# Linear attention and a sine MLP on one core: the first group's work in a new, written-out order, in eight single banks

## The chip, the core and the metric

The kernel runs on one core of a Trainium2 chip. The metric is the device time in microseconds (us), lower is better. The core's engines are TensorE (PE; PEld is its loading of weights), VectorE (DVE), ScalarE (ACT), GpSimd (POOL) and SyncE (SP). They run side by side, each through its own list of instructions in the order in which the program was written, and wait for one another by semaphores. DMA transfers are issued here by SP and by POOL.

## The reference

Two stages follow one another. The first is a causal linear attention with a decay for each head, over 4 batches, 8 heads, 768 positions and 64 values a head. The second is a two-layer MLP with a sine in it, over the resulting 3072 rows of 512 values.

```python
for b in range(nb):                          # blocks along the sequence
    intra = (qb @ kb.T * Dmask) @ vb         # within the block
    inter = (qb * lam_pow) @ kv_state        # from all blocks ahead
    out[:, :, sl] = intra + inter
    kv_state = lam_block * kv_state + (kb * rev_pow).T @ vb
...
x = attn_out, batch by batch, as 3072 x 512
h = x @ w_in                                 # 512 -> 2048
s = sin(alpha * h)
g = h + s * s / (alpha + 1e-9)
out = g @ w_out                              # 2048 -> 512
```

## The kernel before, in words

**Tiling.** The sequence is cut into six chunks of 128 positions. A *unit* u = 4 t + b is chunk t of batch b. The four units of a chunk make a *group* of 512 columns in the tile `xt`, and the MLP is done group by group. The 2048 inner features are 16 *sixteenths* of 128.

**A unit's attention** in the first two chunks: `transposes(u)` turns k and q by PE into PSUM and copies them out by ACT; `scores(u)` multiplies them by eight matmuls into `F_ps`, and DVE multiplies that by the decay mask `Cmask` into `STm`; the outputs are eight matmuls with v (`first_out` in chunk 0, `intra_mm` in chunk 1) plus four with the state `kv` (`inter_mm`, chunk 1 alone); DVE scales them into `xt` (`first_out` or `copy_x`). For the state, POOL decays k (`decay_k`), `state_mm` multiplies it with v, DVE copies the result into `kvs`, POOL casts it into `kv` (`state_put`) and decays it into `kvd` (`state_decay`). From chunk 2 on units are done in pairs: SP transposes k and q by DMA (`pair_transposes`), POOL decays k for both (`pair_decay`), and `pair_scores`, `pair_mask` and `pair_out` follow.

**A sixteenth of the MLP.** `hidden(g, f)` is four matmuls of 512 columns into one bank of PSUM and, on ACT, the sine; the square follows on ACT, or in group 0 on DVE where `on_act` says so (f = 0, 2, 4, 6). `finish(g, f)` is one scalar_tensor_tensor on DVE, which reads the same bank and writes `gall`; only then is the bank free. `project(g, n)` is one of 16 steps of the second layer, four matmuls of 512 columns each; step n works for batch m and a quarter (`part`) of the features and needs a quarter of `w_out`. In a step with part 3 ACT copies the rows out and SP stores them.

**The order.** Nothing is scheduled at run time: each engine's order is that in which the Python code emits. Group 0 is begun by a list of calls behind `spin` (PE kept busy with unused matmuls) and goes on in the main loop over g and i, where `slots(g)` says what of the next chunk's attention is done beside sixteenth i, and `feed(g)` which loads, state casts and decays POOL gets there. Behind the loop's pass g = 0 stand steps 0 to 3 of the projection; from g = 1 on each pass i does `hidden(g, i)` and then a projection step of the group before, four steps ahead (`LEAD`).

**PSUM** has eight banks of 512 float32. In the old kernel the tag `pf` holds a tile of two banks (`F_ps`, also `O_ps` of the pairs and `KVA_ps`); the others (`po`, `pqk`, `ops`, `h0`, `h1`, `h2`) are single. A tile of a tag waits until the last one's readers are done.

Of the kernel before, what the change touches and what calls it, by code (L numbers as in the profile page):

```python
# [14 lines left out]
def kernel(  # L15
# [197 lines left out]
    def transposes(u, tag="pqk"):  # L213
        t, b = divmod(u, B)
        QK_ps = psA.tile([P, 2, HP, T], BF16, name="QK_ps", tag=tag)
        for hp in range(HP):
            nc.tensor.transpose(out=QK_ps[:, 1, hp, :],
                                in_=kn[t][:, b, 2 * hp:2 * hp + 2, :], identity=iden[:])
        for hp in range(HP):
            nc.tensor.transpose(out=QK_ps[:, 0, hp, :],  # L220
                                in_=qn[t][:, b, 2 * hp:2 * hp + 2, :], identity=iden[:])
        QKT = qkp.tile([P, 2, HP, T], BF16, name="QKT")
        nc.scalar.copy(out=QKT[:], in_=QK_ps[:])  # L223
        st[u]["QT"], st[u]["KT"] = QKT[:, 0, :, :], QKT[:, 1, :, :]

    def scores(u, halves=1):
        QT, KT = st[u]["QT"], st[u]["KT"]
        F_ps = psA.tile([P, 2, HP, T], FP32, name="F_ps", tag="pf")
        for hp in range(HP):
            for hd in range(2):  # L230
                nc.tensor.matmul(out=F_ps[:, hd, hp, :],  # L231
                                 lhsT=KT[hd * D:(hd + 1) * D, hp, :],
                                 rhs=QT[hd * D:(hd + 1) * D, hp, :],
                                 start=True, stop=True)
        STm = work.tile([P, 2, HP, T], BF16, name="STm")
        n = HP // halves
        for s in range(halves):
            w = slice(s * n, (s + 1) * n)
            nc.vector.tensor_tensor(out=STm[:, :, w, :], in0=F_ps[:, :, w, :], in1=Cmask[:, :, w, :],  # L239
                                    op=ALU.mult)  # L240
        st[u]["STm"] = STm

    def state_mm(us, tag="pqk"):
        KVA_ps = psA.tile([P, 2, HP, D], FP32, name="KVA_ps", tag=tag)
        for n, u in enumerate(us):
            t, b = divmod(u, B)
            for hp in range(HP):
# [5 lines left out]
        for n, u in enumerate(us):  # L253
            t, b = divmod(u, B)
            kvs[u] = ksp.tile([P, HP, D], FP32, name="kvs")
            if t == 0:
                nc.vector.tensor_copy(out=kvs[u][:], in_=KVA_ps[:, n, :, :])
            else:
                nc.vector.tensor_tensor(out=kvs[u][:], in0=KVA_ps[:, n, :, :], in1=kvd[b][:], op=ALU.add)
# [14 lines left out]
    def intra_mm(u, bank="po"):  # L274
# [42 lines left out]
    def pair_scores(us, tag):  # L317

        F_ps = psA.tile([P, 2, HP, T], FP32, name="F_ps", tag="pf")
        G_ps = [psA.tile([P, HP, D], FP32, name="G_ps", tag=x) for x in ("po", tag)]  # L320
        for hp in range(HP):
            for c in range(2):
                for hd in range(2):
                    for n, u in enumerate(us):
                        w, s = slice(n * D, (n + 1) * D), slice(hd * D, (hd + 1) * D)
                        nc.tensor.matmul(out=G_ps[hd][w, hp, :] if c else F_ps[w, hd, hp, :],  # L326
# [9 lines left out]
    def pair_mask(us):  # L336
        nc.vector.tensor_tensor(out=st[us[0]]["ST"][0][:], in0=st[us[0]]["F_ps"][:], in1=Cmask[:], op=ALU.mult)  # L337

    def pair_out(us, tag):
# [3 lines left out]
        O_ps = psA.tile([P, 2, HP, T], FP32, name="O_ps", tag="pf")  # L343
# [12 lines left out]
        for c in range(2):  # L356
            for hp in range(HP):
                for n in range(2):
                    w = slice(n * D, (n + 1) * D)
                    for hd in range(2):  # L360
                        nc.tensor.matmul(out=O_ps[hd * D:(hd + 1) * D, n, hp, D * c:T],  # L361
                                         lhsT=vn[t][w, 2 * c + b, 2 * hp + hd, :], rhs=ST[c][w, hd, hp, :],
                                         start=(hp == 0 and c == 0), stop=False, skip_group_check=True)
        for n, u in enumerate(us):
            st[u]["O_ps"] = O_ps[:, n]
            for hp in range(HP):
                nc.tensor.matmul(out=O_ps[:, n, hp, :], lhsT=kv[u % B][:, hp, :, :], rhs=st[u]["QT"][:, hp, :],  # L367
                                 start=False, stop=(hp == HP - 1), skip_group_check=True)
            if tag:
                st[u]["K_ps"] = K_ps[n]  # L370

    def sum_state(u):
        if "K_ps" in st[u]:
            kvs[u] = ksp.tile([P, HP, D], FP32, name="kvs")
            nc.vector.tensor_tensor(out=kvs[u][:], in0=st[u]["K_ps"][:], in1=kvd[u % B][:], op=ALU.add)
# [7 lines left out]
    def on_act(g, f):  # L383
        return f % 2 == 1 or f > 7 if g == 0 else True

    FIRST = "h0 h2 po h1 ops h0 h2 h1 ops".split()

    def h_tag(g, f):
        return f"h{(g * NFC + f) % 3}"

    begun = {}

    def hidden(g, f, start_only=False):


        tag = FIRST[f] if g == 0 and f < len(FIRST) else h_tag(g, f)
        parts = [slice(0, GRP)]
        if (g, f) in begun:
            hps, parts = begun.pop((g, f)), [slice(GRP // 2, GRP)]
        else:  # L400
            hps = psA.tile([P, GRP], FP32, name="hps", tag=tag)
        if start_only:
            begun[g, f], parts = hps, [slice(0, GRP // 2)]
        for w in parts:
            for c in range(NDC):
                nc.tensor.matmul(out=hps[:, w], lhsT=w_in_of[f][:, c, :],  # L406
                                 rhs=xt[g][:, c, w], start=(c == 0), stop=(c == NDC - 1))
        if start_only:
            return
        s_sb = mlps.tile([P, GRP], BF16, name="s_sb")  # L410
        nc.scalar.activation(out=s_sb[:], in_=hps[:], func=ACTF.Sin, scale=alpha_sb[:, f:f + 1])  # L411
        s2 = mlps.tile([P, GRP], BF16, name="s2")
        if on_act(g, f):
            nc.scalar.activation(out=s2[:], in_=s_sb[:], func=ACTF.Square)  # L414
        hps_of[g, f] = (hps, s_sb, s2)

    def finish(g, f):
        hps, s_sb, s2 = hps_of.pop((g, f))
        if not on_act(g, f):
            nc.vector.tensor_tensor(out=s2[:], in0=s_sb[:], in1=s_sb[:], op=ALU.mult)  # L420
        nc.vector.scalar_tensor_tensor(out=gall[g][:, f, :], in0=s2[:], scalar=r_sb[:, f:f + 1],  # L421
                                       in1=hps[:], op0=ALU.mult, op1=ALU.add)
# [7 lines left out]
    def project(g, n):  # L430
        m, part = ORDER[n]
        if part == 0:
            ops_of[g, m] = psA.tile([P, DM], FP32, name="ops", tag=("ops", "pqk")[m % 2])
# [36 lines left out]
    def first_out(u, tag, hps_=range(4)):  # L470
# [6 lines left out]
        w = slice(hps_[0], hps_[-1] + 1)  # L477
        nc.vector.tensor_tensor(out=xt[0][:, w, u * T:(u + 1) * T], in0=O_ps[:, w, :],
# [8 lines left out]
    def half_T(u, nm, tag):  # L487

        src = {"KT": kn, "QT": qn}[nm]
        X_ps = psA.tile([P, HP, T], BF16, name="X_ps", tag=tag)  # L490
        for hp in range(HP):
            nc.tensor.transpose(out=X_ps[:, hp, :], in_=src[0][:, u, 2 * hp:2 * hp + 2, :], identity=iden[:])
        XT = firstp.tile([P, HP, T], BF16, name=nm)
        nc.scalar.copy(out=XT[:], in_=X_ps[:])
        st[u][nm] = XT[:]

    spin(9)
    half_T(0, "KT", "pqk")
    spin(3)
    half_T(0, "QT", "ops")  # L500
    spin(1)
    transposes(1, "po")
    spin(1)
    scores(0)
    a_ps = psA.tile([P, NFC], FP32, name="a_ps", tag="h2")
    nc.tensor.transpose(out=a_ps[:], in_=alpha_fp[:], identity=idf[:])
    for hp in range(HP):
        nc.scalar.activation(out=Etab[:, hp, :], in_=pos_row[:], func=ACTF.Exp, scale=ln_hd[:, hp:hp + 1])
    alpha_sb = consts.tile([P, NFC], FP32, name="alpha_sb")
    nc.vector.tensor_copy(out=alpha_sb[:], in_=a_ps[:])  # L510
    r_sb = consts.tile([P, NFC], FP32, name="r_sb")
    nc.vector.reciprocal(out=r_sb[:], in_=alpha_sb[:])
    spin(2)
    scores(1)
    spin(1)
    transposes(2, "pqk")
    spin(1)
    first_out(0, "po")
    spin(1)
    first_out(1, "h1")  # L520
    spin(1)
    scores(2)
    warm = consts.tile([P, 1], FP32, name="warm")
    nc.scalar.activation(out=warm[:], in_=lnlam[:, 0:1], func=ACTF.Sin)
    spin(1)
    half_T(3, "KT", "ops")
    spin(1)
    half_T(3, "QT", "h2")
    spin(1)
    first_out(2, "po")  # L530
    scores(3, 2)
    spin(3)
    first_out(3, "h1", range(0, 2))
    first_out(3, "ops", range(2, 4))
    hidden(0, 0, True)
    hidden(0, 1, True)


    def part_fo(uf, uo, bank="po"):

        if uo is not None:
            intra_mm(uo, bank)
        if uf is not None:
            scores(uf)
        if uo is not None:
            inter_mm(uo)

    def part_k(us, tag="pqk"):
        state_mm(us, tag)
        for u in us:  # L550
            if u >= B:
                state_put(u)
                state_decay(u)

    def slots(g):

        u = [B * (g + 1) + b for b in range(B)]
        T_, FO = transposes, part_fo
        if g == 0:
            return {}, {3: [(part_k, (0, 1), "pf")], 6: [(part_k, (2, 3), "pf")],  # L560
                    8: [(T_, u[0])], 9: [(T_, u[1], "po")], 10: [(FO, u[0], None)],
                    12: [(FO, u[1], u[0]), (copy_x, u[0])], 13: [(T_, u[2])],
                    14: [(FO, None, u[1]), (T_, u[3], "ops"), (copy_x, u[1])], 15: [(FO, u[2], None)]}, {}
# [24 lines left out]
    def feed(g):  # L588

        u = [B * (g + 1) + b for b in range(B)]  # L590
        if g == 0:
            return {7: [(state_put, 0), (state_put, 1)],
# [91 lines left out]
```

## Time and profile before

| | us |
|---|---|
| three runs | 214.43, 214.48, 215.0 (median 214.48) |
| the profiled execution | 214.55, of which the span of the profile is 212.8 |
| PE busy in the span | 203.8 (96%) |
| ACT, DVE, POOL busy | 146.7, 124.6, 106.0 |
| DVE idle ahead of L421 (finish), mostly for ACT | 63.0 |
| granted clock of PE, mean | 0.996 |

The times given with a row are from the start of the span. A row of the timeline has the start, the duration, the engine, the line, the operation, the tiles out<-in and a count; in brackets stands idle time ahead of it and what ended it. "PE busy" counts a matmul up to its modelled end, so neighbours overlap: four matmuls of a sixteenth show 1.03 us and start 0.86 us ahead of the next. The projection steps (L436) and the sixteenths (L406) make up most of PE's time. Loads by POOL's queue (q0) carry 13.4 MB in 77280 packets.

### The profile page before, as it was taken

What the parts mean: (1) busy time and instruction counts of PE and PEld (TensorE: products, weight loads), DVE (VectorE), ACT (ScalarE), POOL (GpSimd) and SP (SyncE); (2) the same over time, 40 slices, a digit from 0 to 9 for tenths busy, and PEclk for the clock granted to TensorE, in tenths of its full rate; (3) what the DMA queues carried; (4) which work ended last, traced back from release to release, by engine and by line L of the source; (5) the groups of instructions that cost most, each with busy time, mean ns of one, the idle gap of its engine ahead of it and who ended that gap; (6) DMA issues with size and microseconds to landing.
All of it is one profiled execution on the core that took longest, in us unless ns stands there. A gap on an engine that the chain in (4) does not pass through costs nothing.

```text
span 212.8 us, 4607 instructions
## 1 busy us (share of the span) xinstructions
PE 203.8 (96%) x1859; PEld 99.9 (47%) x1859; DVE 124.6 (59%) x193; ACT 146.7 (69%) x235; POOL 106.0 (50%) x148
## 2 busy tenths in 40 slices
PE   7799987999999999999999999999999999999993
PEld 2455444544445454454544454544454544444462
DVE  5686978844648764767644677744757544444200
ACT  4774999539685658767679667679677679878521
POOL 7999999896999999528389017110000000000000
PEclk9999999999999999999999999999999999999998
DMA  5999999999999999994999957951110102011032
GB/s 92 154 166 206 175 170 179 207 179 136 170 202 166 161 189 115 154 162 29 185 137 60 212 80 47 177 124 49 52 49 2 52 0 100 2 52 49 0 113 84
DMA packets 100373, 24.69 MB, mean 116 GB/s; under 512 B 92528, under 2 KB 97408, under 8 KB 100352
## 3 DMA queue, kind: packets, MB, share of 16 engines
q0 software_dynamic: 77280, 13.37, 81.3%
q1 hardware_dynamic: 23072, 11.03, 24.6%
q8 instruction: 14, 0.23, 0.4%
q14 instruction: 7, 0.06, 0.1%
HBM read 27.28 MB, written 6.29 MB: 158 GB/s over the span
## 4 chain that ended last, share of the span: by engine, by line
PE 81%; POOL 10%; DMA 6%; issue 1%; DVE 1%; ACT 0%; POOLq 0%; ACTq 0%
PE ops L436 37%; PE hps L406 34%; DMA qn<-in_q_dram 6%; POOL kn L99 2%; POOL vn L99 2%; PE O_ps L367 2%; POOL kdec L210 2%; POOL w_in L105 2%; PE hps L450 2%; PE O_ps L361 1%; POOL qn L99 1%; PE F_ps L326 1%; PE KVA_ps L352 1%; DVE STm L239 1%; PE O_ps L279 1%
## 5 line engine op out<-in xcount | busy, mean ns | idle before, releaser
L421 DVE SCALAR_TENSOR_TENSOR gall<-s,r_sb,hps 128x512 bf16<-128x512 bf16 x96 | 71.3, 746 | 63.0 <-ACT s L414 62.4
L411 ACT ACTIVATE s_sb<-hps,alpha_sb 128x512 bf16<-128x512 f32 x96 | 65.7, 686 | 46.5 <-PE hps L406 46.5
L406 PE MATMUL hps<-xt,w_in 128*128 128x512 bf16 (+1 forms) x392 | 97.6, 375 | 0.0
L436 PE MATMUL ops<-w_out,gall 128*128 128x512 bf16 x368 | 93.1, 379 | 0.1
L414 ACT ACTIVATE s<-s_sb 128x512 bf16<-128x512 bf16 x92 | 57.9, 630 | 2.9
L406 PEld LDWEIGHTS <-w_in 128*128 128x128 bf16 x392 | 37.4, 98 | 43.5 <-issue 1.7
L436 PEld LDWEIGHTS <-gall 128*128 128x128 bf16 x368 | 34.9, 98 | 39.7 <-DMA w_out<-in_moe_w_out_dram 0.2
L265 POOL CAST kv<-kvs 64x256 bf16<-64x256 f32 x40 | 16.2, 405 | 27.7 <-PE O_ps L367 20.8
L441 ACT COPY o_sb<-ops 128x512 f32<-128x512 f32 x23 | 13.1, 571 | 6.0 <-PE ops L436 6.0
L293 DVE TENSOR_TENSOR xt<-O_ps,Etab 128x512 bf16<-128x512 f32 x20 | 13.6, 686 | 4.2 <-PE O_ps L367 3.3
L95 POOL DMA_DIRECT2D kn<-in_k_dram x16 | 13.3, 848 | 0.0
L99 POOL DMA_DIRECT2D qn<-in_q_dram x10 | 12.9, 1288 | 0.8 <-DMA w_out<-in_moe_w_out_dram 0.8
L95 POOL DMA_DIRECT2D vn<-in_v_dram x16 | 13.2, 845 | 0.0
L302 POOL TENSOR_TENSOR kdec<-kn,Rpair 128x1024 bf16<-128x1024 bf16 x6 | 11.4, 1910 | 1.9 <-DMA kn<-in_k_dram 1.9
L485 PE MATMUL hps<-fill 128*128 128x512 bf16 x26 | 9.9, 476 | 1.5 <-DVE fill L125 1.5
L239 DVE TENSOR_TENSOR STm<-F_ps,Cmask 128x1024 bf16<-128x1024 f32 (+1 forms) x9 | 9.8, 1103 | 1.7 <-PE F_ps L231 1.5
L271 POOL TENSOR_TENSOR kvd<-kvs,L 128x256 f32<-128x256 f32 x16 | 9.8, 614 | 1.0
L337 DVE TENSOR_TENSOR STm<-F_ps,Cmask 128x1024 bf16<-128x1024 f32 x8 | 9.7, 1217 | 0.0
L210 POOL TENSOR_TENSOR kdec<-kn,Rtok 128x512 bf16<-128x512 bf16 x8 | 8.5, 1070 | 0.2
L223 ACT COPY QKT<-QK_ps 128x1024 bf16<-128x1024 bf16 x6 | 6.0, 1000 | 1.0 <-PE QK_ps L220 0.8
L334 DVE TENSOR_TENSOR STm<-G_ps,Cmask 128x256 bf16<-128x256 f32 x16 | 6.0, 419 | 0.6
L99 POOL DMA_DIRECT2D vn<-in_v_dram x6 | 6.0, 1021 | 0.0
(80 smaller groups left out, 115.3 us busy)
## 6 DMA issues: line engine op xcount, KB each, us to landing
out_dram<-o_sb SPq DMA_DIRECT2D x23, 256.0 KB, 2.4
vn<-in_v_dram POOLq DMA_DIRECT2D x20, 128.0 KB, 5.2
kn<-in_k_dram POOLq DMA_DIRECT2D x19, 128.0 KB, 5.9
w_out<-in_moe_w_out_dram POOLq DMA_DIRECT2D x4, 512.0 KB, 14.2
w_in<-in_moe_w_in_dram POOLq DMA_DIRECT2D x3, 512.0 KB, 11.1
qn<-in_q_dram POOLq DMA_DIRECT2D x3, 512.0 KB, 8.9
qn<-in_q_dram POOLq DMA_DIRECT2D x4, 256.0 KB, 12.4
w_in<-in_moe_w_in_dram POOLq DMA_DIRECT2D x2, 256.0 KB, 6.8
```

The source lines that it names most:

```text
L95: nc.gpsimd.dma_start(out=dst[t][n * D:(n + 1) * D, 2 * c:2 * c + 2, :, :].rearrange("p b h e -> p (b h) e"), in_=src[2 * n:2 * n + 2, :, ...
L99: nc.gpsimd.dma_start(out=dst[t][:, b0:b1, :, :].rearrange("p b h e -> p (b h) e"), in_=src[b0:b1, :, t * T:(t + 1) * T, :].rearrange("b h ...
L210: nc.gpsimd.tensor_tensor(out=kdec[:], in0=kn[t][:, b, :, :], in1=head_bc(Rtok), op=ALU.mult)
L239: nc.vector.tensor_tensor(out=STm[:, :, w, :], in0=F_ps[:, :, w, :], in1=Cmask[:, :, w, :], op=ALU.mult)
L265: nc.gpsimd.tensor_copy(out=kv[b][s, :, hd, :], in_=kvs[u][s, :, :])
L293: nc.vector.tensor_tensor(out=xt[t][:, :, b * T:(b + 1) * T], in0=st[u]["O_ps"], in1=Etab[:], op=ALU.mult)
L406: nc.tensor.matmul(out=hps[:, w], lhsT=w_in_of[f][:, c, :], rhs=xt[g][:, c, w], start=(c == 0), stop=(c == NDC - 1))
L411: nc.scalar.activation(out=s_sb[:], in_=hps[:], func=ACTF.Sin, scale=alpha_sb[:, f:f + 1])
L414: nc.scalar.activation(out=s2[:], in_=s_sb[:], func=ACTF.Square)
L421: nc.vector.scalar_tensor_tensor(out=gall[g][:, f, :], in0=s2[:], scalar=r_sb[:, f:f + 1], in1=hps[:], op0=ALU.mult, op1=ALU.add)
L436: nc.tensor.matmul(out=ops[:], lhsT=gall[g][:, f, m * P:(m + 1) * P], rhs=w_out_sb[part][:, f % 4, :], start=(f == 0), stop=(f == NFC - 1))
L441: nc.scalar.copy(out=o_sb[:], in_=ops[:])
```

## The change

1. The whole of group 0, its attention, chunk 1's attention, the states of chunk 0 and the first seven projection steps, is written as one string, `FILL`, of 168 entries. A loop emits them one by one; the helpers are split so that an entry is one engine's piece (matmuls, copy, mask, sine, square, finish). So the order on each engine is the string's.
2. All eight banks are single: `pf` becomes `pfa` and `pfb`, and each entry names its bank. `scores` and the pairs' `F_ps` and `O_ps` become lists of two tiles; a mask becomes two instructions of 128x512.
3. Sixteenths 0, 1 and, of group 1, 0, 1 and 2 (entries 16, 17, 18) are done in two halves of 256 columns: `Ha`, when the first two batches of `xt` are there, and `Hb`.
4. Which square goes to which engine changes: in group 0 nine on ACT and seven on DVE (0, 2, 3, 6, 7, 11, 12) for twelve and four; those of 16, 17 and 18 on DVE. Two of the four state copies of chunk 0 go to ACT.
5. POOL gets the four `w_out` loads ahead of all eight state casts (four of the eight stood ahead of them). The decays, the loads of chunk 2 and all behind it keep their order. SP's order is unchanged.
6. The main loop starts with g = 1; in it the passes i = 0, 1, 2 emit only their feeds, as their sixteenths and projection steps are in `FILL`. The banks of the later sixteenths rotate in another order (`h_tag`).

```diff
-    def scores(u, halves=1):
+    def scores(u, banks):
...
-        F_ps = psA.tile([P, 2, HP, T], FP32, name="F_ps", tag="pf")
+        F_ps = [psA.tile([P, HP, T], FP32, name="F_ps", tag=x) for x in banks]
...
+    def mask(u, w=slice(0, 4)):
+        for hd in range(2):
+            nc.vector.tensor_tensor(out=st[u]["STm"][:, hd, w, :], in0=st[u]["F_ps"][hd][:, w, :],
+                                    in1=Cmask[:, hd, w, :], op=ALU.mult)
...
+    def first_state(u, on_scalar):
+        kvs[u] = ksp.tile([P, HP, D], FP32, name="kvs")
+        (nc.scalar.copy if on_scalar else nc.vector.tensor_copy)(out=kvs[u][:], in_=st[u]["K_ps"])
...
     def pair_mask(us):
-        nc.vector.tensor_tensor(out=st[us[0]]["ST"][0][:], in0=st[us[0]]["F_ps"][:], in1=Cmask[:], op=ALU.mult)
+        for hd in range(2):
+            nc.vector.tensor_tensor(out=st[us[0]]["ST"][0][:, hd], in0=st[us[0]]["F_ps"][hd][:], in1=Cmask[:, hd],
+                                    op=ALU.mult)
...
-    def on_act(g, f):
-        return f % 2 == 1 or f > 7 if g == 0 else True
...
+    def hidden_mm(g, f, tag, w=slice(0, GRP)):
+
+        if tag:
+            hps_of[g, f] = psA.tile([P, GRP], FP32, name="hps", tag=tag)
+        for c in range(NDC):
+            nc.tensor.matmul(out=hps_of[g, f][:, w], lhsT=w_in_of[f][:, c, :],
+                             rhs=xt[g][:, c, w], start=(c == 0), stop=(c == NDC - 1))
...
+    FILL = """
+        Et F0:pfa,pfb spin2 M0 F1:po,ops Tk2:h2 spin3 Tq2 spin1 M1 cp2 I0:ops spin2 I1:h2 F2:po,pqk Tk3:h1
+        spin1 ck3 X1 Tq3:pfb spin3 M2 cq3 F3:h1,h2 X0 Mb3 I2:pfb spin3 Ma3 Ha1:po X2 Ib3:ops warm Ia3:h2
+        Ha0:pfa Xa3 AT:pfb Xb3 al Hb1 Hb0 H3:pqk sin1 sqA1 Z1 sin0 H2:h0 sin2 wout sqD2 sqD0 K2:pfb H4:ops
+        H6:h1 sin3 sqD3 Z0 H5:po ksA3 sin4 ksA2 sin6 Z2 sqA4 H7:pfb H8:pfa sin5 Z3 sqD6 Z4 sin7 Tk5:pqk
+        Tk4:ops sqA5 K0:h2 Tq5 sqD7 Z6 Z5 Z7 sin8 sqA8 Z8 cp5 Tq4 H10:h0 cp4 ksD0 put0 H11:po ksD1
+        F5:pfa,pfb sin11 F4:ops,pqk sin10 M5 H13:h1 H14:h2 put1 sin13 sqD11 sqA13 sqA10 M4 sin14 H15:pfa
+        sin15 I5:pqk Z11 Z13 sqA15 sqA14 I4:ops J5 J4 H9:pfb Tk7:h1 X5 Tk6:po Tq7 Tq6 X4 Ha18:pqk put3 cp7
+        Z15 Ha17:pfa Z14 cp6 sin9 F7:h2,ops Z10 H12:h1 F6:h0,po put2 sqA9 M7 I7:ops M6 P0:h2 I6:h0 Z9 J7 J6
+        X7 Ha16:pfb sin12 X6 sqD12 P1:po Hb17 Hb16 Z12 Hb18 sin17 P2 P3 sin16 sqD17 Z17 sqD16 sin18 sqD18
+        Z16 P4 P5 Z18 P6
+    """
...
+    rest = """decay 4, load 0 0, decay 5, load 0 2, kvd 0, load 1 0, kvd 1, decay 6, load 1 2, kvd 2, decay 7, kvd 3"""
...
-    for g in range(NT + 1):
-        if g < NT:
+    for g in range(1, NT + 1):
+        if 1 < g < NT:
...
+            if g == 1 and i < 3:
+                continue
```

The entries: F scores, M mask (Ma, Mb halves), T transposes of k or q, cp, ck and cq their copies, I the outputs' matmuls with v, J those with the state, X the scaling into `xt`, H a sixteenth's matmuls, sin and sq its sine and square (A on ACT, D on DVE), Z its finish, K the states of two units, ksA and ksD their copies, put the casts, P a projection step, wout the four loads, AT and al alpha, Et the powers, warm the loading of the sine's table.

More of the change, by code (lines that the diff above doesn't have):

```diff
@@ L234, in scores, with state_mm @@
                                  start=True, stop=True)
[L235 to L243, printed above, removed]
+        st[u]["F_ps"] = F_ps
+        st[u]["STm"] = work.tile([P, 2, HP, T], BF16, name="STm")
+    def mask(u, w=slice(0, 4)):
+        for hd in range(2):
+            nc.vector.tensor_tensor(out=st[u]["STm"][:, hd, w, :], in0=st[u]["F_ps"][hd][:, w, :],
+                                    in1=Cmask[:, hd, w, :], op=ALU.mult)
+    def state_mm(us, tag):
         KVA_ps = psA.tile([P, 2, HP, D], FP32, name="KVA_ps", tag=tag)
@@ L417, in finish @@
-    def finish(g, f):
[L418 to L422, printed above, removed]
+        return ("h2", "h1", "h0")[(g * NFC + f) % 3]
+    def hidden_mm(g, f, tag, w=slice(0, GRP)):
[4 more added lines that the diff above has]
+                             rhs=xt[g][:, c, w], start=(c == 0), stop=(c == NDC - 1))
@@ L424, with hidden @@
+    def hidden(g, f):
+        hidden_mm(g, f, h_tag(g, f))
+        sine(g, f)
+        square(g, f)
+    def finish(g, f):
+        nc.vector.scalar_tensor_tensor(out=gall[g][:, f, :], in0=s2_of.pop((g, f))[:], scalar=r_sb[:, f:f + 1],
+                                       in1=hps_of.pop((g, f))[:], op0=ALU.mult, op1=ALU.add)
     ops_of = {}
@@ L493, in half_T, with copy_half, powers @@
+    def copy_half(u, i):
+        nm = ("KT", "QT")[i]
         XT = firstp.tile([P, HP, T], BF16, name=nm)
-        nc.scalar.copy(out=XT[:], in_=X_ps[:])
+        nc.scalar.copy(out=XT[:], in_=st[u]["X_ps", i][:])
         st[u][nm] = XT[:]
+    def powers():
+        for hp in range(HP):
+            nc.scalar.activation(out=Etab[:, hp, :], in_=pos_row[:], func=ACTF.Exp, scale=ln_hd[:, hp:hp + 1])
+    alpha_sb = consts.tile([P, NFC], FP32, name="alpha_sb")
+    r_sb = consts.tile([P, NFC], FP32, name="r_sb")
@@ L497 @@
+    gall[1] = gbp.tile([P, NFC, GRP], BF16, name="gall")
+    new_xt(1)
     spin(9)
-    half_T(0, "KT", "pqk")
+    half_T(0, 0, "pqk")
+    copy_half(0, 0)
     spin(3)
-    half_T(0, "QT", "ops")
+    half_T(0, 1, "ops")
+    copy_half(0, 1)
     spin(1)
-    transposes(1, "po")
+    transposes(1, 0, "po")
+    transposes(1, 1)
+    copy_T(1)
     spin(1)
-    scores(0)
-    a_ps = psA.tile([P, NFC], FP32, name="a_ps", tag="h2")
-    nc.tensor.transpose(out=a_ps[:], in_=alpha_fp[:], identity=idf[:])
@@ L507 @@
[L507 to L546, printed above, removed]
@@ new lines, with at_group @@
+    """
+    half = (slice(0, GRP // 2), slice(GRP // 2, GRP))
+    two = (slice(0, 2), slice(2, 4))
+    def at_group(f):
+        return divmod(f, NFC)
+    DO = {
+        "spin": lambda n: spin(n), "Et": powers, "AT": alpha_T, "al": alpha_in, "warm": sine_table,
+        "wout": lambda: [load_w_out(i) for i in range(4)],
+        "ck": lambda u: copy_half(u, 0), "cq": lambda u: copy_half(u, 1), "cp": copy_T,
+        "Tk": lambda u, x: half_T(u, 0, x) if u == 3 else transposes(u, 0, x),
+        "Tq": lambda u, x=None: half_T(u, 1, x) if u == 3 else transposes(u, 1),
+        "F": lambda u, *x: scores(u, x), "M": mask,
+        "Ma": lambda u: mask(u, two[0]), "Mb": lambda u: mask(u, two[1]),
+        "I": lambda u, x: first_out(u, x) if u < B else intra_mm(u, x),
+        "Ia": lambda u, x: first_out(u, x, range(0, 2)), "Ib": lambda u, x: first_out(u, x, range(2, 4)),
+        "J": inter_mm, "X": lambda u: first_x(u) if u < B else copy_x(u),
+        "Xa": lambda u: first_x(u, two[0]), "Xb": lambda u: first_x(u, two[1]),
+        "Ha": lambda f, x: hidden_mm(*at_group(f), x, half[0]), "Hb": lambda f: hidden_mm(*at_group(f), None, half[1]),
+        "H": lambda f, x: hidden_mm(*at_group(f), x), "sin": lambda f: sine(*at_group(f)),
+        "sqA": lambda f: square(*at_group(f)), "sqD": lambda f: square(*at_group(f), False),
+        "Z": lambda f: finish(*at_group(f)),
+        "K": lambda u, x: state_mm((u, u + 1), x), "ksA": lambda u: first_state(u, True),
+        "ksD": lambda u: first_state(u, False), "put": state_put,
+        "P": lambda n, x=None: project(0, n, x),
+    }
@@ L611, in feed @@
                 14: [(Tr, t, 1), (pair_decay, nxt)]}
-    for g in range(NT + 1):
-        if g < NT:
+    rest = """decay 4, load 0 0, decay 5, load 0 2, kvd 0, load 1 0, kvd 1, decay 6, load 1 2, kvd 2, decay 7, kvd 3"""
+    entries = FILL.split()
+    last = max(n for n, e in enumerate(entries) if e[:3] in ("put", "wou"))
+    for n, entry in enumerate(entries):
+        if entry == "P6":
+            for a in feed(1)[0]:
+                a[0](*a[1:])
+        do(entry)
+        if n == last:
+            for a in rest.split(", "):
+                op, *x = a.split()
+                if op == "decay":
+                    decay_k(int(x[0]))
+                elif op == "kvd":
+                    state_decay(int(x[0]))
+                else:
+                    load_one(2, int(x[0]), int(x[1]), int(x[1]) + 2)
+    for g in range(1, NT + 1):
+        if 1 < g < NT:
             gall[g] = gbp.tile([P, NFC, GRP], BF16, name="gall")
```

155 lines of the change are left out of this document (62 added, 93 removed).

## The prediction

> **What bounds the kernel now.** I read the page first (busy shares, slices), then the windows by stage, the timeline of PE, POOL and DVE, and last the DMA issues with their times to landing.
>
> ```profile
> PE   7799987999999999999999999999999999999993
> POOL 7999999896999999528389017110000000000000
> DMA  5999999999999999994999957951110102011032
> ```
>
> The windows by stage (length, then busy time of PE, its weight loads, DVE, ACT and POOL, the granted clock, the DMA share and GB/s):
>
> ```profile
> 15.00:45.00 30.00, 27.30 (x261) 14.63 (x258) 23.65 (x37) 21.03 (x33) 28.48 (x36) 1.00 1.68 189
> 45.00:50.00 5.00, 5.00 (x25) 2.28 (x24) 1.82 (x3) 3.36 (x6) 4.64 (x11) 1.00 2.44 158
> 50.00:205.00 155.00, 155.00 (x1446) 73.74 (x1445) 88.75 (x134) 110.95 (x177) 59.07 (x82) 1.00 0.89 101
> ```
>
> From 45 us to 205 us PE has no idle time at all, and the change leaves that work and nearly all its order alone. So it can only win ahead of 45 us: the whole rest moves earlier by what the start saves, unless something in it does not move. What may not move is the DMA stream: its slices (5.3 us each) stand at 9 tenths up to about 95 us.
>
> The timeline of PE (start, duration):
>
> ```profile
> 49.90 1.03 PE L406 MATMUL hps<-xt,w_in 128*128 128x512 bf16 x4
> ...
> 66.50 0.45 PE L352 MATMUL KVA_ps<-vn,kdec 64*64 64x64 bf16 x32
> 66.77 0.52 PE L361 MATMUL O_ps<-STm,vn 64*64 64x128 bf16 x32
> ```
>
> That of POOL:
>
> ```profile
> 30.80 1.73 POOL L265 CAST kv<-kvs 64x256 bf16<-64x256 f32 x4
> ...
> 52.23 3.76 POOL L302 TENSOR_TENSOR kdec<-kn,Rpair 128x1024 bf16<-128x1024 bf16 x2 [1.92 <-DMA kn<-in_k_dram]
> 55.93 3.31 POOL L95 DMA_DIRECT2D vn<-in_v_dram  x4
> ```
>
> And the DMA issue that starts at 58.40, the last of the four v loads of chunk 2, with its time to landing:
>
> ```profile
> vn<-in_v_dram POOLq DMA_DIRECT2D x1, 128.0 KB, 7.9
> ```
>
> 49.90 is hidden(1, 3), the first step after everything that the change touches: both kernels have done the same work when PE gets there. 66.50 is the first use of v of chunk 2, in pair_out of the first pair. The last v load lands at 58.40 + 7.9 = 66.3, and PE comes to it 0.2 us later. That distance decides this change.
>
> **Part 1: the order of the first group.** I add up by starting intervals, taken from rows: on ACT sine to sine 0.58, sine to its square 0.71, square to the next 0.54, a copy of 128x1024 0.89; on DVE the scalar_tensor_tensor 0.66 (three in 2.06), xt 0.60 (two in 1.29), a square 0.34, or 0.45 ahead of its own use, a state copy 0.33; on PE a sixteenth 0.864 (49.90 to 50.76).
>
> Up to the first full sixteenth little is won. In eight single banks scores(1) no longer waits for the mask of batch 0, but the batch-3 masks become four pieces of 128x256. The nearest row is the 128x256 mask of L334, 0.419; its step lies between a quarter of the 1.22 row's 1.13 (0.28) and 0.42, taken as 0.34. The outputs of batch 1 take the bank that the copy of batch 2's Q and K leaves at 12.5; eight matmuls (0.35, and 0.17 to the result) put xt of 1 at 13.1 and the mask of batch 2 at 13.70. From there DVE has 1.20 + 0.60 (xt of 0) + 1.36 (masks of 3) + 0.60 (xt of 2) + 0.36 + 0.42 (the halves of batch 3): 18.25, against 18.02 before. The whole masks of 1.22 become two steps of 0.60 (the 128x512 row has 0.68 each, two in 1.28): nothing, to 0.14 more each.
>
> From there PE has to do, to the end of P6: 14 sixteenths and 8 halves (0.44 each) 15.6; seven projection steps 6.05; eight transposes of 0.22, scores 0.33, the two parts of the outputs 0.35 and 0.22, each four times, and two states of 0.37, 6.1: 27.8 us from 18.3, so 46.1 without a wait. (Six halves more than before cost a start each, 0.01 by 0.44 against 0.432.) Its waits in the new order, by the same rows: K2 for kdec at 21.06, 0.20; Q of chunk 1 (landings 27.20 and 35.53) 0.64 and 0.32; DVE and ACT ahead of I5, F7 and I7 0.64. Sum 1.8, so P6 ends at 47.9. DVE has 21 us of work (16 finishes 10.6, masks 4.8, squares 2.6, xt 2.4, state copies 0.7) from its first finish at 20.3 and ends the sixteenths' part at 43.2; ACT has 18.5 us from 18.9 (16 sines 9.4, squares 4.9, copies 3.6 and 0.7): three squares leave it (9 for 12), two state copies come. No row has that copy on ACT: between half of a 128x512 copy (0.29) and a whole one (0.59), 0.33 taken; ACT waits over 3 us for sin17 anyway, which covers either. The floor is P6 itself: the last w_out load (issued at 30.01, 16.9 us to landing) is there at 46.88, so P6 ends no earlier than 47.8. The same adding-up on the old order gives 49.66 where the trace has 49.90; with these 0.24 the new start ends at 48.1. **The start saves 49.90 - 48.1 = 1.8 us** (bounds 0 and 2.1).
>
> **Part 2: loads.** SP's queue keeps its order. On POOL the four w_out loads go ahead of the eight state copies. That brings no landing forward: the stream works through its requests in the order of issue, with 154 to 207 GB/s in every slice of 5.3 us up to 48 us, and those ahead of w_out are untouched. The k loads of chunk 2 are issued 1.8 us later (after eight copies in a row from 30.8 instead of four), but at 37 they still take 14.8 us to land, so their place stays near 51.9 and the transposes by SP that wait for them stay too: the last (55.77, 4.8) lands at 60.6. PE would ask for it, with pair_scores (62.36), at 60.56: no loss.
>
> **Part 3: where the saving goes.** With everything on PE 1.8 us earlier, pair_out would begin at 64.7. Its first half (c = 0) needs v pieces that are there; the second needs the piece of 66.3. PE then waits some 1.6 us, the whole queue of sixteenths behind it, and goes on at 66.34 (a landing releases PE in 0.04: 39.09 to 39.13). Before, this point was 66.50 + 0.12 = 66.62. **What is left is 0.28 us.** Nothing behind it waits less: PE is full, and the split of F_ps and O_ps into two banks adds 8 masks of 2 x 0.68 for 1.22 on DVE, which idles 63 us ahead of the scalar_tensor_tensor.
>
> **Part 4: does v stay at 66.3?** It hangs on POOL: k of chunk 2 (51.9), two kdec of 1.9, then the v issues. In the old order POOL is ready for kdec at 50.31 and waits 1.92. In the new one four copies (1.81 with their gap) come in between, and 0.78 of it falls into a wait for w_out that then vanishes: 50.31 + 1.03 = 51.34, 0.9 ahead. Against it stand DVE's squares: five (11, 12, 16, 17, 18) now run between 31 and 46 beside POOL's work; the old order has none there. The copies of 25.61 with one square beside them took 2.02, those of 30.80 without one 1.73: 0.29 a square, or 0.23 by kdec's 1.26 against 1.04. Five cost 1.2 to 1.45, so kdec starts at 52.5 to 52.8 and v comes 0.3 to 0.55 late; as one or two squares will meet a DMA issue instead, I take 0.2. The 0.28 shrink to about 0.1.
>
> The Trainium skill, "SBUF — State Buffer", section "Who interferes with whom", says that a VectorE instruction with two SBUF inputs and a GpSimd instruction that reads SBUF exclude each other for a whole instruction. The copy row shows 0.29 for a square of 0.42, some two thirds of that. By the rule as it stands the result is the third rival below.
>
> **The sum.** Profiled execution 214.55 (span 212.8) - 0.1 = 214.4; the three runs' median is 214.48, so 214.4 holds against it too.
>
> **Rivals.** (1) *The start's saving is kept.* That needs v of chunk 2 to land 1.6 us earlier, or PE's wait to fall on less than it seems. For it: PE is idle nowhere in the trace behind 45 us, and three stores share the stream with v (57 to 66). Against it: their sum of bytes is the same. 214.55 - 1.8 = 212.7, in part 213.5. (2) *The change does not do what it says*: DVE is filled almost without a gap from 22 to 43, and late masks hold PE until 49.9. Then nothing is won: 214.5. (3) *Slower: POOL misses its slack.* If each of the five squares holds POOL for its full 0.42, kdec starts at 51.34 + 2.1 = 53.44 and v lands at 67.5: PE goes on at 67.55 for 66.62, 215.4. It decides from 52.5 on; beyond 53.1 it is more than 0.3%.
>
> **How the numbers follow.** 0.3%, about what a measurement of this kernel tells from no change, is 0.64 us: 213.84 to 215.12. Forecast (214.1 to 214.8) 0.55; rival 1 0.19; rival 2 0.08; rival 3 and any later v 0.18. So faster 0.19, same 0.63, slower 0.18. The range leaves out the better half of rival 1 and the worse half of rival 3: 213.4 to 215.4.
>
> **What would show it.** Right: hidden(1, 3) begins near 48.1; P6 near 47.2, just behind the last w_out; POOL's first kdec of pairs at 52.2 to 52.8; the last v piece lands at 66.3 to 66.8, and PE has an idle 1.4 to 2 us in pair_out, put down to vn. Wrong: no such gap and pair_out at 65 (rival 1); hidden(1, 3) at 49.5 or later (rival 2); kdec beyond 53 (rival 3).

## The result, and the profile after

The changed kernel is faster: 213.13 us median of 6 executions (212.62 to 213.80) against 214.74 us of the kernel before beside them, a ratio of 0.9927 with a 95% interval of 0.9905 to 0.9950, so about 1.6 us. Three more sets of the same kernel gave 0.9924 (0.9903 to 0.9945), 0.9934 (0.9916 to 0.9952) and 0.9947 (0.9930 to 0.9965). The forecast was 214.4 in a range of 213.4 to 215.4: too high, 213.13 lies below the range, and the likeliest case was the wrong one. All ratios here are of fast executions; slow ones, over 1.5% above the fastest of their kernel, are only seven of the twelve of e_held. The profiled execution took 213.48 (span 211.8), 1.07 less than the 214.55 of before.

The page's slices of after show no change of kind. PE is full from about 50 us, the DMA engines up to about 95 us:

```profile
PE   7999998999999999999999999999999999999993
POOL 7999969998999999528299026200000000000000
DMA  4999999999999999996969939951110102011032
```

The windows by stage, with the columns as in the prediction:

```profile
15.00:45.00 30.00, 28.62 (x278) 16.61 (x283) 26.48 (x48) 22.47 (x36) 27.87 (x35) 1.00 1.68 189
45.00:50.00 5.00, 4.95 (x24) 2.29 (x24) 3.49 (x6) 1.54 (x3) 4.64 (x10) 1.00 2.49 157
50.00:205.00 155.00, 153.08 (x1421) 73.80 (x1442) 88.33 (x141) 109.22 (x175) 60.12 (x83) 1.00 0.89 101
```

Between 15 and 45 us PE does 28.62 us of work instead of 27.30: the start is denser. From 50 to 205 us it was busy for all of the 155.00 us, and now for 153.08. Part of the missing 1.92 is real waiting; part is matmul records that this trace lacks (1421 matmuls listed, 1446 before). The timeline tells them apart: start, duration, what, and in brackets idle time with what ended it.

```profile
47.95 1.03 PE L392 MATMUL hps<-xt,w_in 128*128 128x512 bf16 x4
...
60.42 0.24 PE L325 MATMUL F_ps<-QT,KT 64*64 64x128 bf16 x1
60.93 0.25 PE L325 MATMUL F_ps<-QT,KT 64*64 64x128 bf16 x3 [0.27 <-DMA QT<-qn]
...
65.06 0.34 PE L353 MATMUL KVA_ps<-vn,kdec 64*64 64x64 bf16 x18
65.57 0.31 PE L353 MATMUL KVA_ps<-vn,kdec 64*64 64x64 bf16 x14 [0.17 <-DMA vn<-in_v_dram]
...
66.17 0.62 PE L368 MATMUL O_ps<-QT,kv 128*128 128x128 bf16 x8
```

The first row is hidden(1, 3), at 49.90 before: the start saves 1.95. PE then stops twice, in pair_scores for a transpose of q and in pair_out for v. From the first L325 row to the first L368 row it needs 5.75 us here, and 4.86 in the kernel before (62.36 to 67.22), which does not wait: 0.89 us of waiting. So 67.22 becomes 66.17, 1.05 earlier, and that is the whole gain of this execution (1.07): behind that row both need the same 147.3 us.

The chain of waits (start, length, what) shows who is late:

```profile
38.42 13.02 DMA kn<-in_k_dram
...
51.75 3.76 POOL kdec L301 x2
55.51 2.41 POOL vn L95 x3
57.92 7.61 DMA vn<-in_v_dram
65.53 0.04 issue
65.57 0.31 PE KVA_ps L353 x14
```

The last v piece is issued at 57.92 and lands 7.61 later, at 65.53. The forecast put it at 66.3 to 66.8.

### The profile page after: what moved, and what is told of

Its sections match the earlier page's. It is cut to its first block, busy times and chain, and to the rows that moved or that the text cites. A ratio compares the mean times of both kernels' runs of the same rounds, so it can differ in the third digit from the quotient of the medians.

```text
span 211.8 us, 4627 instructions
## 1 busy us (share of the span) xinstructions
PE 202.9 (96%) x1844; PEld 101.1 (48%) x1874; DVE 127.8 (60%) x214; ACT 143.3 (68%) x231; POOL 106.5 (50%) x148
## 4 chain that ended last, share of the span: by engine, by line
PE 66%; DMA 16%; POOL 13%; issue 2%; DVE 1%; ACT 0%; POOLq 0%; ACTq 0%
PE ops L430 30%; PE hps L392 28%; DMA w_in<-in_moe_w_in_dram 6%; DMA kn<-in_k_dram 6%; DMA vn<-in_v_dram 4%; PE O_ps L368 2%; POOL kn L99 2%; POOL kdec L301 2%; PE hps L444 2%; POOL kv L264 2%; POOL vn L99 2%; PE O_ps L362 1%; POOL w_in L105 1%; POOL qn L99 1%; PE F_ps L325 1%
## 5 line engine op out<-in xcount | busy, mean ns | idle before, releaser
L392 PE MATMUL hps<-xt,w_in 128*128 128x512 bf16 (+1 forms) x395 | 96.4, 368 | 0.9
L430 PE MATMUL ops<-w_out,gall 128*128 128x512 bf16 x349 | 90.1, 379 | 0.8 <-issue 0.2
L392 PEld LDWEIGHTS <-w_in 128*128 128x128 bf16 x404 | 38.5, 98 | 43.3 <-issue 1.4
L405 ACT ACTIVATE s<-s_sb 128x512 bf16<-128x512 bf16 x86 | 53.9, 629 | 2.6
L95 POOL DMA_DIRECT2D vn<-in_v_dram x16 | 13.2, 846 | 0.0
L241 DVE TENSOR_TENSOR STm<-F_ps,Cmask 128x512 bf16<-128x512 f32 (+1 forms) x18 | 10.3, 624 | 1.6 <-PE F_ps L232 1.6
L337 DVE TENSOR_TENSOR STm<-F_ps,Cmask 128x512 bf16<-128x512 f32 x16 | 10.2, 682 | 0.0
L224 ACT COPY KQT<-QK_ps 128x1024 bf16<-128x1024 bf16 x6 | 5.9, 1011 | 2.1 <-PE QK_ps L219 2.0
L376 DVE TENSOR_TENSOR kvs<-KVA_ps,kvd 128x256 f32<-128x256 f32 x16 | 6.5, 419 | 1.0 <-DVE gall L415 0.4
```

Of the source, the lines that this page charges most:

```text
L95: nc.gpsimd.dma_start(out=dst[t][n * D:(n + 1) * D, 2 * c:2 * c + 2, :, :].rearrange("p b h e -> p (b h) e"), in_=src[2 * n:2 * n + 2, :, ...
L392: nc.tensor.matmul(out=hps_of[g, f][:, w], lhsT=w_in_of[f][:, c, :], rhs=xt[g][:, c, w], start=(c == 0), stop=(c == NDC - 1))
L430: nc.tensor.matmul(out=ops[:], lhsT=gall[g][:, f, m * P:(m + 1) * P], rhs=w_out_sb[part][:, f % 4, :], start=(f == 0), stop=(f == NFC - 1))
```

## The experiments

The reading above leaves two views. Theory A: v lands a fixed time behind its issue, so the chain k, kdec, v sets a floor and the start's saving is lost down to it. Theory B: PE alone sets the end. After the first four runs came theory C: the DMA engines are full, and v and the transposed q land when the bytes beside them are through.

**The same kernel again** (r_after, beside the next three runs).

> The changed kernel once more, for how its landings differ from one execution to the next. Theory A (the end is set by a chain beside TensorE: k of chunk 2 lands, GpSimd decays it, issues the v loads, and pair_out waits for the last of these): the time is 213.1 as measured, less than the kernel before by 1.6; in the profile the last piece of k of chunk 2 lands near 51.4 and the last piece of v near 65.5, and where an execution has them later, its span is longer by the same amount. Theory B (TensorE's own work alone sets the end, and the start's 1.95 us counts in full): the time varies with no relation to these landings, and with them 0.5 later the span stays.

212.97 median. Its profiled execution took 214.09, and the chain of waits there names another transfer:

```profile
55.37 6.49 DMA QT<-qn
```

The second transpose of q landed at 61.86; PE stood 1.1 us in pair_scores and then found v (66.12) there. Which of the two transfers is late changes from one execution to the next, and so does the sum: 0.89 in the first, 1.33 in this one. Theory B's claim that the landings do not matter falls.

**More work on PE** (e_spin4): `+ spin(4)` behind the fillers of the start.

> The changed kernel with four more unused matmul groups (0.86 us of TensorE work) right behind the fillers of the start, ahead of hidden(1, 3), whose result nothing reads. Theory A: TensorE waited 0.9 us in all for transposed q and k and for v in pair_scores and pair_out, and the added work lies in that slack, so the time is 0 to 0.2 above the changed kernel's. Theory B: 0.86 above it.

214.04, which is 1.07 above r_after (ratios to before 0.9988, 0.9970 to 1.0006, and 0.9924): as theory B has it, and not absorbed as theory A has it. In its profiled execution pair_scores did not wait and pair_out did, 0.74 in all, with v at 65.92. That execution is 0.40 above the first one of the changed kernel (213.88 for 213.48) and below r_after's (214.09), so it does not decide. Why the executions without a profile do not absorb the added work is shown by no row that I have, and stays open.

**POOL later** (e_late):

```
+ for _ in range(2): nc.gpsimd.tensor_tensor(out=idle, in0=Cmask[:, 0], in1=Cmask[:, 0], op=mult)
  (ahead of the first pair_decay of chunk 2)
```

> The changed kernel with two idle GpSimd multiplies (about 2.1 us by the width of its decay tables' multiplies) ahead of the first decay of k of chunk 2, and TensorE's work as it was. Theory A: v's loads are issued 2.1 us later and land near 67.6, so TensorE waits 1.6 to 2.1 longer in pair_out and the time is 1.6 to 2.1 above the changed kernel's. Theory B: 0 to 0.3 above it.

213.81, 0.84 above r_after, half of what A forecast. POOL's timeline shows the multiplies and the v loads pushed back:

```profile
52.40 2.17 POOL L302 TENSOR_TENSOR idle<-Cmask 128x512 bf16<-128x512 f32 x2
54.53 3.76 POOL L305 TENSOR_TENSOR kdec<-kn,Rpair 128x1024 bf16<-128x1024 bf16 x2
58.23 3.31 POOL L95 DMA_DIRECT2D vn<-in_v_dram  x4
```

The last v load was issued at 60.70, 2.7 later than in r_after (58.01), and landed at 66.12, at the very same time. Issued late, v needs 5.4 us instead of 8.1. This is where theory A fails: the landing does not follow the issue. (This execution's start was also 0.75 later at pair_scores, so its time says less than its landing.)

**v loads first** (e_vfirst):

```
- 2: [(pair_decay, p), (pair_decay, q_)], 4: [(load_one, 2, 2)],
+ 2: [(load_one, 2, 2), (pair_decay, p), (pair_decay, q_)], 4: [],
```

> The changed kernel with GpSimd's v loads of chunk 2 issued ahead of its two decays of k instead of behind them, so that v lands some 6 us earlier. Theory A: the wait in pair_out (0.2 to 0.4) is gone; the waits for transposed q and k in pair_scores (0.5) stay, so the time is 0.2 to 0.4 below the changed kernel's, unless the v transfers now hold back the transposes, which would add to pair_scores up to 1. Theory B: within 0.1 of it.

216.88, 1% above before (ratio 1.0102, 1.0086 to 1.0119), where neither theory had it. v landed at 61.89, and the price was paid by the transposes of q beside it: the second landed at 62.28, and PE waited for it. The groups of waits of PE, and three windows of it:

```profile
PE F_ps L325 <- DMA QT<-qn: 2.2, 1, 2.2
```

```profile
62.00:64.00 2.00, 1.67 (x35) 0.84 (x35) 1.03 (x3) 0.00 (x0) 2.00 (x3) 0.73 0.98 319
64.00:66.00 2.00, 2.00 (x6) 0.73 (x5) 1.57 (x3) 0.00 (x0) 2.00 (x3) 0.50 1.95 124
66.00:68.00 2.00, 2.00 (x9) 0.74 (x7) 0.26 (x1) 1.32 (x2) 1.85 (x4) 0.92 2.17 138
```

The wait is 2.2 us, yet pair_out is reached 4.05 late (8.91 us from L325 to L368 instead of 4.86): behind the gap the granted clock is 0.50, and a sixteenth takes twice its time.

**Three stores held back, on ACT** (e_held, and e_before_held for the kernel before): stores of blocks 0 to 2 of group 0 are collected and issued by `nc.scalar.dma_start` behind pair_out of the first pair.

> The changed kernel with the first three output stores of group 0 (three of 256 KB, issued at 56.7, 57.6 and 58.9) held back: they are issued by ScalarE behind pair_out of the first pair. Theory A (v lands a fixed 7.6 us behind its issue at 57.9): v still lands near 65.5, and the time stays within 0.15 of the changed kernel's. Theory C (the DMA engines are full, and v lands when the bytes ahead of it and beside it are through, 0.75 MB less here, some 3.9 us at 200 GB/s): the last piece of v lands near 62 to 63 and the second transpose of q by 60.6 or earlier, TensorE waits at most 0.3 in all, and the time is 0.3 to 0.6 below the changed kernel's, with less spread.

> The same holding back of three stores in the kernel before, where TensorE comes to pair_scores and pair_out 1.9 us later and waits for neither. Theory C: v lands 3 to 4 us earlier and nobody waits for it, so the time is within 0.15 of the kernel before (and its runs near 215.0 become rarer, if they are runs with a late landing). If it gains 0.3 or more, the kernel before was held by these landings too, and the start's saving is not what made the change faster.

v landed at 62.56, as C has it, and pair_out was reached without a wait (L368 at 64.95). But the kernels came out at ratios to before of 1.0041 (1.0001 to 1.0081; its executions spread from 213.57 to 223.17) and 1.0067 (1.0042 to 1.0093, 215.83). Behind the row of O_ps<-QT,kv their profiled executions need 148.6 and 148.8 us instead of 147.3. The new place was bad: in e_before_held's timeline of ACT the three issues stand in a row, and the next sine starts 1.28 late:

```profile
68.65 1.81 ACTq L456 DMA_DIRECT2D out_dram<-o_sb  x3
70.51 0.69 ACT L411 ACTIVATE s_sb<-hps,alpha_sb 128x512 bf16<-128x512 f32 x1 [1.28 <-issue]
```

So these two show the landing, and not what it is worth in time. What takes e_held up to 223 is open.

**POOL later in the kernel before** (e_before_late).

> The kernel before with two idle GpSimd multiplies (about 2.1 us) ahead of its first decay of k of chunk 2. Theory A: v is issued and lands 2.1 us later, 66.3 becomes 68.4, TensorE waits 1.8 to 1.9 in pair_out: 1.8 to 1.9 above the kernel before. Theory C: v waits for the DMA engines anyway and lands by 66.9: 0 to 0.5 above it. TensorE alone: 0.

214.66, ratio 1.0002 (0.9990 to 1.0015). The expectation of A overlooked that POOL waits 1.92 for k there (its row in the prediction), which hides the idle multiplies nearly whole: v was issued at 58.32, as without them. So the time tells nothing between A and C, only that POOL had that slack. The landing tells something: v, issued at 58.32 instead of 58.40, landed at 63.90 instead of 66.29. In this execution k landed earlier (50.68 for 51.93), and the first two stores were issued at 56.02 and 56.66 instead of 57.17 and 58.09. The same issue with other neighbours lands 2.4 us earlier, which a fixed time behind the issue cannot give.

**Without the early halves** (e_whole): `Ha16 Ha17 Ha18 ... Hb16 Hb17 Hb18` become `H17:pfa H16:pfb H18:pqk` behind X6.

> The changed kernel without its early halves: hidden sixteenths 16, 17 and 18 are made whole, behind output 6, so that TensorE has less to do while it waits for masks. The start ends some 1.3 us later by the rows. Theory A with a fixed v (65.5 to 66.3): 0.4 above the changed kernel, the rest of the 1.3 having been waited for. Theory C and TensorE alone: 0.9 to 1.3 above it, as the landings come early in most executions.

214.02, ratio 0.9973 (0.9960 to 0.9987): by the ratios 0.9 above the changed kernel, whose four sets have 0.9933 in the mean, as theory C and PE alone have it. The halves of the second group, with their early place, bring a good half of the gain. PE reached pair_scores at 61.58 (60.42 in after) and waited for nothing.

**Without three stores** (e_nostore, e_before_nostore): `if g or m == 3:` ahead of the store.

> The changed kernel without the first three output stores of group 0 (their 0.75 MB are left out for good, so three blocks of the output stay unwritten); every other instruction is as it was. Theory C (v and the transposed q land when the DMA engines have the bytes beside them through): v's last piece lands near 62.5, TensorE waits for it no more and for q at most 0.3; the time is what the start saves in full, 1.9 below the kernel before: 212.4 to 212.6. Theory A (v lands a fixed time behind its issue): as the changed kernel, 212.9 to 213.1.

> The kernel before without the same three stores. Theory C: TensorE waited for nothing there, so 214.3 to 214.5, as the kernel before; the difference to the changed kernel without them is then the start's saving alone, 1.8 to 2.0. If it gains 0.3 or more itself, later transfers (chunk 3) held the kernel too.

211.96 (ratio 0.9895, 0.9874 to 0.9915) and 214.19 (0.9997, 0.9981 to 1.0012). This is the run that decides. PE's timeline of the changed kernel without the stores:

```profile
64.24 0.45 PE L353 MATMUL KVA_ps<-vn,kdec 64*64 64x64 bf16 x32
64.51 0.52 PE L362 MATMUL O_ps<-STm,vn 64*64 64x128 bf16 x32
64.97 0.62 PE L368 MATMUL O_ps<-QT,kv 128*128 128x128 bf16 x8
```

The 32 matmuls of L353 are one row with no bracket. v's last piece was issued at 57.72, hardly earlier than in after, and landed at 63.33, which is 2.1 to 3.7 ahead of the four profiled executions of the changed kernel (65.44 to 67.06); in the kernel before it went from 66.29 to 63.29, by 3.0. The kernel before gains at most 0.4 from the stores' absence, since nobody waits there; the changed one gains 1.3 against its set on the same chip (213.29). Some 0.3 of it has nothing to do with v: behind the row of O_ps<-QT,kv both kernels without stores need 147.0 us instead of 147.3, and both came out below what theory C expected. The difference of the two, 2.2 us, is free of that: it is what the start saves when nothing takes it back.

The Trainium skill, "DMA: Bandwidth & Descriptors", section "Queues, rings and completion order", says that each DMA engine takes turns between its queues, packet by packet. The landings agree: v on POOL's queue, its first piece issued at 55.45 in after, is held back by stores on SP's queue that are issued from 56.69 on.

**The stores behind chunk 3's transposes, on SP** (e_held_sp), **an idle multiply ahead of v** (e_lead), **both** (e_best), with the changed kernel beside them (r_after2, r_after3):

```
+ 12: [(Tr, 3, 1), (store_held,)],           (e_held_sp, e_best; nc.sync.dma_start)
+ 4: [(idle_once,), (load_one, 2, 2)],       (e_lead, e_best; one multiply, 1.04 us)
```

> A candidate: the changed kernel with the same three stores issued by SyncE behind its transposes of chunk 3, near 80, instead of near 57. Theory C: the waits of chunk 2 are gone (v near 62.5), and the 0.75 MB now stand beside the v loads of chunk 3 and the k loads of chunk 4, whose users come over 5 us behind their landings: 212.4 to 212.7. If chunk 3's landings are as tight as chunk 2's, it is no better than the changed kernel or up to 1 worse.

> The changed kernel again on the same chip as the runs beside it: median 212.9 to 213.2, and a profiled execution in which TensorE waits between 0 and 1.2 us in all for the transposed q and v of chunk 2; what it waits and what its span is above 210.9 go together.

> The changed kernel with one idle GpSimd multiply (1.09 us) between its second decay of k of chunk 2 and the first v load, so that SyncE's last transpose of q is issued 1.2 us or more ahead of v instead of 0.15 to 0.6. Theory C with a race (the transpose is slow because v's packets join it): the transpose lands 3.2 behind its issue, near 58 to 58.5, and TensorE waits for v alone, which lands at 66 to 67 behind the three stores: 212.9 to 213.5, about as the changed kernel. Theory A (v a fixed time behind its issue): 1.1 above it, 214.1.

> Both: the three stores by SyncE behind its transposes of chunk 3, and the idle multiply ahead of v. Theory C with the race: the transpose lands near 58, v near 64, TensorE waits at most 0.2: 212.0 to 212.3, near the kernel without those stores (212.0). If chunk 3's landings hold the kernel instead: 212.7 and above. Theory A: 214.1.

> The changed kernel on the chip of the two runs beside it: median 212.9 to 213.3, single executions from 212.3 to 215.

e_held_sp: 212.74 (0.9918, 0.9897 to 0.9939), r_after2 213.29; e_lead 213.21 (0.9944, 0.9921 to 0.9967), r_after3 213.40; e_best 212.38 (0.9897, 0.9882 to 0.9912), its five executions within 212.25 and 212.51, just above its 212.0 to 212.3. e_held_sp alone is 0.55 below r_after2, but their intervals overlap, and in its profiled execution PE still waited 0.6 in all, for the transposed q (landing 61.24). e_best beats the changed kernel by 1.0, with intervals apart, and the one before by 2.05. Whether the idle multiply adds anything to the moved stores is not shown, as the intervals of e_best and e_held_sp overlap too. PE's timeline there has no wait:

```profile
64.35 0.45 PE L354 MATMUL KVA_ps<-vn,kdec 64*64 64x64 bf16 x32
64.62 0.52 PE L363 MATMUL O_ps<-STm,vn 64*64 64x128 bf16 x32
65.08 0.62 PE L369 MATMUL O_ps<-QT,kv 128*128 128x128 bf16 x8
```

v landed at 63.61. The idle multiply alone gains nothing, since v still stands among the stores (65.27, 0.97 us of waiting). The race that I supposed between the transpose of q and v is not borne out: with v's first load 1.7 us behind it in e_lead the transpose still took 4.63 us, and with 0.63 in e_nostore 3.14. What makes it 3.1 in some executions and up to 6.5 in others stays open.

The slowest execution of the changed kernel is r_after2's profiled one, 215.05, where v's last piece landed at 67.06 and PE waited 2.4 us in all, twice the most that was expected:

```profile
64.69 0.31 PE L353 MATMUL KVA_ps<-vn,kdec 64*64 64x64 bf16 x14
65.54 0.22 PE L353 MATMUL KVA_ps<-vn,kdec 64*64 64x64 bf16 x2 [0.54 <-DMA vn<-in_v_dram]
67.11 0.31 PE L353 MATMUL KVA_ps<-vn,kdec 64*64 64x64 bf16 x14 [1.34 <-DMA vn<-in_v_dram]
```

The four profiled executions of the changed kernel and those that tell the causes apart (waiting: first L325 row to first row of O_ps from QT and kv, less 4.86; the last column is the time of the execution less the one ahead of it):

| execution | last q transpose, issue to landing | last v piece, issue to landing | waiting | O_ps<-QT,kv at | rest |
|---|---|---|---|---|---|
| before (214.55) | 55.77 to 60.59 | 58.40 to 66.29 | 0 | 67.22 | 147.33 |
| after (213.48) | 55.30 to 60.89 | 57.92 to 65.53 | 0.89 | 66.17 | 147.31 |
| r_after (214.09) | 55.37 to 61.86 | 58.01 to 66.12 | 1.33 | 66.76 | 147.33 |
| r_after2 (215.05) | 55.32 to 60.10 | 58.41 to 67.06 | 2.41 | 67.70 | 147.35 |
| r_after3 (213.38) | 54.94 to 59.66 | 58.27 to 65.44 | 0.87 | 66.07 | 147.31 |
| e_late (214.08) | 54.95 to 58.05 | 60.70 to 66.12 | 0.58 | 66.76 | 147.32 |
| e_nostore (211.95) | 54.62 to 57.76 | 57.72 to 63.33 | 0 | 64.97 | 146.98 |
| e_best (212.38) | 55.09 to 59.79 | 59.14 to 63.61 | 0 | 65.08 | 147.30 |

In all rows but e_nostore, where stores are left out, the rest is the same within 0.05 us. So the time of these executions is decided by when PE gets through pair_out, and by nothing behind it.

## Why the prediction was wrong, step by step

**The start (part 1): right.** 48.1 forecast, 47.95 measured; 1.8 forecast, 1.95 measured. The column of O_ps<-QT,kv less the waiting gives 65.2 to 65.4 in all four executions of the changed kernel, 1.8 to 2.0 ahead of 67.22. The parts of the sum are not confirmed as well as the sum: from 18.3 to 48 us PE is shown idle for 0.8 to 1.0 us (busy 28.74 to 28.87 of 29.70 in r_after, r_after2 and r_after3), where 1.8 of waits was added up, and busy for some 1.0 more than the 27.8 of the sum. A short wait can hide under a matmul's modelled end, so it stays open whether work or waits were mis-sized; the two differences cancel, which is luck.

**Loads (part 2): nearly right.** The last w_out load landed at 46.83 (46.88 before), as forecast. The second transpose of q was forecast at 60.6, with PE there at 60.56 and "no loss". A margin of 0.04 was put at nothing. The transpose landed at 59.66 to 61.86, and in two of four executions PE waited for it, once for 1.1. This cost had to have bounds.

**POOL (part 4): right in place, its squares half as dear.** kdec was forecast at 52.5 to 52.8 by the sum, and at 52.2 to 52.8 in all. It started at 51.75 and 51.84 where k was last, at 52.24 and 52.10 where POOL was. A square beside a POOL instruction cost POOL 0.25 in the eight copies (in after 3.79 for twice 1.73 and a gap of 0.08) and 0.17 to 0.20 in kvd (in after 0.80 for 0.63) and kdec (in r_after2 1.24 for 1.04), and only two or three of the five show such a loss: 0.4 to 0.6 in all, not 1.2 to 1.45. The third rival, kdec beyond 53, did not come; v at 67.06 did, once, by way of the stream. The prediction had the loss on POOL's side alone. The larger one fell on DVE, as rows of after show, where a square that meets nothing takes 0.42:

```profile
43.84 0.63 POOL L270 TENSOR_TENSOR kvd<-kvs,L 128x256 f32<-128x256 f32 x1
43.86 1.89 DVE L407 TENSOR_TENSOR s<-s_sb 128x512 bf16<-128x512 bf16 x1
44.42 1.04 POOL L210 TENSOR_TENSOR kdec<-kn,Rtok 128x512 bf16<-128x512 bf16 x1
45.42 0.80 POOL L270 TENSOR_TENSOR kvd<-kvs,L 128x256 f32<-128x256 f32 x1
```

The square lasted through two POOL multiplies that run at their usual length, and only the third is longer. That agrees with the rule of the Trainium skill that I weighed ("SBUF — State Buffer", "Who interferes with whom"), an exclusion for a whole instruction: which engine pays for it hangs on which started first.

**Where the saving goes (part 3): the step that failed.** "What is left is 0.28 us" took one landing, 66.3, from one execution, and made it a floor. The mechanism was right in this: three of the four profiled executions wait in pair_out for vn (in r_after the wait for q, ahead of it, hides that for v), and the waits are all that the start loses. But the term is not one number: v landed at 65.53, 66.12, 67.06 and 65.44. PE's wait measured 0.89, 1.33, 2.41 and 0.87 in all, for v and for q together, where the sum had 1.5 to 1.7 for v and nothing for q, so that these four keep 1.05, 0.46, -0.48 and 1.15 of the start's saving where the sum kept 0.1. And the executions without a profile were faster still: their median over the four sets is 213.1 (20 executions, 212.3 to 214.0), where 214.43 - 1.95 = 212.5 would be no wait at all. That leaves about 0.6 of waiting in them, which is inferred and not seen.

**Rival 1 is what happened, in part,** at 213.1 in its 212.7 to 213.5. Its sign, pair_out at 65 with no gap, shows only in the kernels with the stores moved or left out; the changed kernel keeps part of its saving where v lands earlier than 66.3, as in three of the four profiled executions. I named its lever, three stores that share the stream with v, and set it aside because "their sum of bytes is the same". The sum is the same, but who stands among whom is not fixed by it: without those stores v lands 2.1 to 3.7 us earlier and the whole start is kept (e_nostore), and e_late's v, issued 2.7 later, lands no later. The 7.9 us from issue to landing were a queue, not a latency. A term that is a queue needed a range of at least the 3 us of those stores, and rival 1 more than 0.19.

## What to carry to other kernels

Where the DMA engines are full, an issue-to-landing time of one profile is no constant: it changes with what other queues put beside the transfer, so give it a range and look for the transfers beside it that nobody waits for. When PE gets earlier to data that a full stream brings, moving the stores out of that stretch is worth more than issuing the load earlier; here the moved stores, with an idle multiply ahead of v, gave 1.0 us (0.55 without it, which the intervals do not tell from nothing), while issuing v earlier lost 3.9. And where a store is moved to, ask who is queued behind its issue: on ACT it held the sines, on SP behind the transposes it held nobody (a rest of 147.30 in e_best).

## What the runs showed of the hardware that was not expected

A gap of 2.2 us in PE's work (e_vfirst) was followed by a granted clock of 0.50 for some 3.4 us, and the kernel took 3.9 us more; gaps of 0.54 and 1.34 close together (r_after2) left the clock at 1.00. The Trainium skill, "TensorE: Matmul & The Clock Gate", section "What's actually happening", gives a window of about 3.4 us of idleness for that; here 2.2 was enough.

The second transpose of q by DMA, the same bytes each time, took 3.1 to 6.5 us from issue to landing (7.9 beside early v loads).
